# Softmax denominators over slots computed on VectorE through 32x32 block transposes, in a kernel of memory attention and a maxout feed-forward layer

## The chip, the cores and the metric

The kernel runs on one core of a Trainium2 chip. A core has TensorE (PE, matrix products into PSUM), VectorE (DVE), ScalarE (ACT), GpSimd (POOL) and SyncE (SP); each works through its own queue in order and waits for others by semaphores. Here POOL's queue issues nearly all loads and SP's queue the stores. The metric is the device time of one execution in microseconds; lower is better.

## The reference

Each of 8 x 8 (batch, head) pairs has 576 positions, 64 features and 32 memory slots. Weights over positions (`a`) gather keys and values into the 32 slots; queries then attend to the slots. The result, as 4608 tokens of 512 features, goes through a layer with the maximum of three products.

```python
a = np.exp(phi - np.max(phi, axis=2, keepdims=True))
a = a / (np.sum(a, axis=2, keepdims=True) + 1e-09)
k_m = np.einsum('bhsm,bhsd->bhmd', a, k)
v_m = np.einsum('bhsm,bhsd->bhmd', a, v)
scores = scale * np.matmul(q, k_m.transpose(0, 1, 3, 2))
attn = np.exp(scores - np.max(scores, axis=-1, keepdims=True))
attn = attn / (np.sum(attn, axis=-1, keepdims=True) + 1e-09)   # over the 32 slots
x = np.matmul(attn, v_m)                                       # then (4608, 512)
h = np.maximum(np.maximum(x @ w1, x @ w2), x @ w3)
out = h @ w_out
```

## The kernel before

The whole kernel is one list of steps, written out by hand in the text at the end of the function (lines 509 to 530) and emitted in that order. A step is a letter, an index and a batch, such as F6@1; a "!" at its end swaps the engine that empties its PSUM buffer, VectorE for ScalarE or the reverse (table EVAC, line 137). Every engine takes its own instructions from the list in that order. Pools decide when a buffer can be written again: four PSUM buffers of two banks serve all products, and k and v have one buffer for even and one for odd batches.

The algebra is rearranged: with x = attn v_m, the product x @ w1 is attn (v_m w1), so v_m is multiplied with the weights first ("fold"), and attn, already laid out with slots on partitions, is multiplied with that. The maximum with x @ w3 is taken by subtracting w3 from w1 and w2 beforehand and adding w3 w_out back at the end.

The steps, for batch b:

- H, L: loads of k, v (L94), phi (L90), q (L102). Y: weights (L108, L115). I: identity matrix on GpSimd. Z: warm-up products of zeros (L132).
- E: exponential of phi, ScalarE, L203. B: the gathering of keys and values into slots, 72 products for k and v of 32-wide tiles (L216); batch 1 splits it in B0 and B1. N: reciprocal and normalising on VectorE (L232, L236, L246). K: transposes of the result (L261).
- Q: queries transposed in 32x32 blocks on VectorE (L273), in two halves. S: scores (L295), then two exponentials on ScalarE, g = 0 and g = 1, into tile e2 (L304), where 128 partitions are four heads of 32 slots each.
- M: denominators, by a product with a block matrix of ones, so that every partition gets the sum of its 32 slots (L316). R: 1/sum as exp(-ln(sum)) on ScalarE (L329, L335). X: the product of e2 with it on VectorE, into tile attn (L340). All three once for each g.
- W, O, V: the transposed w3, the product w3 w_out and the differences of the weights, once (L157, L165, L186).
- D: the folds (L361), evacuated into wp; D3 goes with w3 w_out. F: twelve products per batch of attn with wp (L387); the even ones pass through a ReLU on ScalarE (L143), the odd ones through a maximum on VectorE (L400). T: the output product (L418, L427; T4 covers the seam of two batches, L436), a copy of PSUM to SBUF (L145 or L149) and a store.

Of the kernel before, what the change touches and what calls it, by code (L numbers as in the profile page):

```python
# [8 lines left out]
FP32 = mybir.dt.float32  # L9
BF16 = mybir.dt.bfloat16  # L10
AF = mybir.ActivationFunctionType
ALU = mybir.AluOpType
# [3 lines left out]
def kernel(  # L16
# [12 lines left out]
    nc = tc.nc  # L29

    B, H, S, D = q.shape
    M = phi.shape[-1]
    P = 128
    NP = H // 2
    NG = NP // 2
    HP = P // 2
    NC = S // HP
    R = 32
# [3 lines left out]
    SH = S // 2  # L42
    BANK = 512

    const = ctx.enter_context(tc.tile_pool(name="const", bufs=1))
    inp = ctx.enter_context(tc.tile_pool(name="inp", bufs=2))
    work = ctx.enter_context(tc.tile_pool(name="work", bufs=2))
# [3 lines left out]
    acc_pool = ctx.enter_context(  # L51
        tc.tile_pool(name="accp", bufs=4, space=bass.MemoryType.PSUM)
    )
# [28 lines left out]
    def load_ph(b):  # L82
        ph = inp.tile([P, NP, NC, M], FP32, name="ph")
        loaded.setdefault(b, {})["ph"] = ph
        dst = ph.rearrange("p j c m -> p j (c m)")
        if b == 0:
            for h in halves:
                nc.sync.dma_start(out=dst[:, h], in_=by_pair(phi, b)[:, h])
        else:
            nc.gpsimd.dma_start(out=dst, in_=by_pair(phi, b))  # L90

    def load_kv(b, i, h=slice(0, NP)):
        kv = loaded.setdefault(b, {})["kv"] = kvos[b % 2]
        nc.gpsimd.dma_start(  # L94
            out=kv[:, i, h].rearrange("p j c d -> p j (c d)"),
            in_=by_pair((k, v)[i], b)[:, h],
        )

    def load_q(b):
        qq = inp.tile([P, NP, NC, D], BF16, name="qq")  # L100
        loaded.setdefault(b, {})["q"] = qq
        nc.gpsimd.dma_start(  # L102
            out=qq.rearrange("p j c d -> p j (c d)"), in_=by_pair(q, b)
        )

    def load_w(i):
        w = (moe_w1, moe_w2, moe_w3)[i]
        nc.gpsimd.dma_start(  # L108
            out=w_sb[:, :, i], in_=w.rearrange("(j p) f -> p j f", p=P)
        )  # L110
# [3 lines left out]
    def load_wo():  # L114
        nc.gpsimd.dma_start(out=wo_sb, in_=moe_w_out.rearrange("(t p) c -> p t c", p=P))  # L115
# [3 lines left out]
    warm = const.tile([P, BANK], BF16, name="warm")  # L119
    nc.vector.memset(warm, 0.0)  # L120
    nc.vector.memset(kvos[0][:, 2], 1.0)
    blkones = const.tile([P, P], BF16, name="blkones")
    nc.vector.memset(blkones, 0.0)
    for i in range(P // M):
        nc.vector.memset(blkones[M * i : M * (i + 1), M * i : M * (i + 1)], 1.0)
    nc.vector.memset(kvos[1][:, 2], 1.0)

    def warm_up(n):
# [68 lines left out]
    st = {}  # L197

    def att_exp(b, js=slice(0, NP)):
        s = st.setdefault(b, {})  # L200
        if "e" not in s:
            s["e"] = work.tile([P, NP, NC, M], BF16, name="e")
        nc.scalar.activation(out=s["e"][:, js], in_=loaded[b]["ph"][:, js], func=AF.Exp)  # L203

    def att_kv(b, part=None):
        s = st[b]
        kvp = acc_pool.tile([P, NG, BANK], FP32, name="kvp", tag="acc")
        s["kvp", part] = kvp
        kv = loaded[b]["kv"]
        cols = {None: slice(0, 3), 0: slice(0, 3, 2), 1: slice(1, 2)}[part]  # L210
        nd = {None: 3 * D, 0: 2 * D, 1: D}[part]
        for c in range(NC):
            for j in range(NP):
                for a in range(NG):
                    r = slice(HP * a, HP * (a + 1))
                    nc.tensor.matmul(  # L216
                        kvp[M * j : M * (j + 1), a, 0:nd],
                        lhsT=s["e"][r, j, c, :],
                        rhs=kv[r, cols, j, c, :],
                        start=(c == 0),  # L220
                        stop=(c == NC - 1),
                        tile_position=(HP * a, M * j),
                    )
# [54 lines left out]
    attns = {}  # L278
# [29 lines left out]
                scale=0.125,  # L308
            )

    def att_sum(b, g):
        s = st[b]
        e2 = s["e2"]
        sm = acc_pool.tile([P, 2, BANK], FP32, name="sm", tag="acc")
        for h in range(2):
            nc.tensor.matmul(  # L316
                sm[:, h, 0:SH],
                lhsT=blkones,
                rhs=e2[:, g, h * SH : (h + 1) * SH],
                start=True,  # L320
                stop=True,
            )
        s["sm", g] = sm

    def att_rec(b, g):
        s = st[b]
        sm = s["sm", g]
        ln = work.tile([P, S], FP32, name="ln")
        nc.scalar.activation(  # L329
            out=ln.rearrange("p (h n) -> p h n", h=2),  # L330
            in_=sm[:, :, 0:SH],
            func=AF.Ln,
        )
        r = work.tile([P, S], FP32, name="r")
        nc.scalar.activation(out=r, in_=ln, func=AF.Exp, scale=-1.0)  # L335
        s["r", g] = r

    def att_mul(b, g):
        s = st[b]
        nc.vector.tensor_tensor(  # L340
            out=attns[b // 2][:, g, (b % 2) * S : (b % 2 + 1) * S],
            in0=s["e2"][:, g, 0:S],
            in1=s["r", g],
            op=ALU.mult,
        )

    wps, wp3s = {}, {}
# [134 lines left out]
    def issue(b, n, swap):  # L482

        i = int(n[1:]) if len(n) > 1 else None
        {
            "I": lambda: make_identity(nc, ident),
            "Y": lambda: load_w(i) if i < 3 else load_wo(),
            "L": lambda: load_ph(b) if i == 0 else load_q(b) if i == 3 else load_kv(b, i - 1),
            "H": lambda: load_kv(b, i % 2, halves[i // 2]),
            "E": lambda: [att_exp(b, h) for h in (halves if b == 0 else [slice(0, NP)])],  # L490
            "B": lambda: att_kv(b, i),
            "N": lambda: att_kv_norm(b, i),
            "K": lambda: att_kv_t(b, swap, i),
            "Q": lambda: att_q(b, i),
            "S": lambda: att_score(b),
            "M": lambda: att_sum(b, i),
            "R": lambda: att_rec(b, i),
            "X": lambda: att_mul(b, i),
            "D": lambda: fold(b, i, swap),
            "F": lambda: ffn1(b, i, swap),  # L500
            "T": lambda: ffn2(b, i, swap),
            "W": lambda: w3_t(i, swap),
            "O": lambda: w3_o(i, swap),
            "V": lambda: w_diff(i),
            "Z": lambda: warm_up(i),
        }[n[0]]()


    for w in """
        H3@0 H2@0 H1@0 H0@0 L3@0 E@0 Z48@0 B@0 Y2@0 N@0 Y3@0 Q0@0 Q1@0 I@0 Z4@0 K@0! Z8@0 S@0  # L510
        Z6@0 M1@0 R1@0 Y0@0 Y1@0 L0@1 M0@0 R0@0 W2@0 W1@0 W0@0 Z9@0 O0@0 X0@0 O1@0 X1@0 O2@0
        O3@0 L1@1 V1@0 V0@0 D1@0 D0@0! L3@1 D3@0 V2@0 F8@0 F10@0 F4@0 V4@0 F2@0 D2@0! F6@0!
        D4@0 F0@0 F3@0 F1@0 E@1 F5@0 F7@0 L2@1 F9@0 F11@0 B0@1 N0@1 T3@0 Q0@1 L1@2 L0@2 K0@1!
        T1@0 Q1@1 S@1 B1@1 N1@1 M0@1 L2@2 R0@1 K1@1 M1@1 X0@1 T0@0 R1@1 D1@1! L3@2 D0@1 D2@1
        E@2 X1@1 T2@0 F6@1! F10@1 F8@1 F7@1 F11@1 F0@1 F1@1 D3@1 B@2 F4@1 N@2 F9@1 L1@3 F5@1
        K@2! F2@1 Q1@2 F3@1 D3@2 L0@3 D2@2 T4@1! Q0@2 S@2 T0@1 M1@2 E@3 R1@2 M0@2 R0@2 T1@1!
        D0@2 L2@3 X1@2 D1@2! B@3 T2@1! L3@3 X0@2 L1@4 N@3 L0@4 F2@2 F6@2 Q1@3 Q0@3 F4@2 K@3
        F10@2 F0@2 F3@2 S@3 L2@4 F1@2 F8@2 L3@4 F11@2 M1@3 F7@2 R1@3 D3@3 E@4 D0@3! F9@2 T3@1
        F5@2 M0@3 R0@3 B@4 D2@3 D1@3! X1@3 N@4 L0@5 X0@3 T0@2! F0@3 F2@3 Q1@4 F4@3 Q0@4 L2@5
        F10@3 K@4 F6@3 F11@3 E@5 F3@3 D1@4! D0@4 T2@2! S@4 L1@5 F7@3 F8@3 F1@3 M0@4 F5@3 F9@3  # L520
        R0@4 X0@4 M1@4 R1@4 B@5 N@5 X1@4 D2@4 L3@5 D3@4 Q0@5 T2@3! K@5 F6@4 L3@6 F0@4 Q1@5 F4@4
        F7@4 S@5 F5@4 L0@7 F2@4 Q1@6 L0@6 Q0@6 F8@4 M1@5 R1@5 F1@4 E@7 F9@4 T1@2 F3@4 M0@5 R0@5
        L1@6 E@6 F10@4 T1@3 T3@3 X1@5 X0@5 F11@4 D3@5 D0@5 L2@6 B@6 D1@5! T0@3! N@6 L1@7 F2@5
        L2@7 F4@5 K@6 T4@3! S@6 B@7 D2@5 N@7 F3@5 F8@5 L3@7 F0@5 Q0@7 M0@6 R0@6 F1@5 T0@4! M1@6
        Q1@7 K@7 R1@6 T3@2 X0@6 X1@6 S@7 F5@5 F10@5 F6@5 F9@5 M1@7 R1@7 F7@5 X1@7 F11@5 M0@7
        R0@7 T3@4 X0@7 D2@7! D2@6 D0@7 T4@5! D1@6 D0@6 D1@7! T0@5! F0@7 F8@6 F4@6 F0@6 F6@6
        F9@6 F1@7 F10@6 F5@6 F11@6 F2@7 F6@7 F7@6 F2@6 F1@6 D3@6 D3@7 T1@4 F4@7 F3@6 F5@7 F3@7
        F8@7 F10@7 F11@7 F9@7 F7@7 T3@6 T1@5 T2@5! T2@7! T1@6 T0@7! T1@7 T2@6! T0@6! T2@4! T3@5
        T4@7! T3@7
    """.split():  # L530
        n, b = w.rstrip("!").split("@")
        issue(int(b), n, w.endswith("!"))
# [30 lines left out]
```

## Time and profile before

| what | us |
|---|---|
| median of 13 runs | 170.94 |
| lowest, highest | 170.37, 171.69 |
| the profiled execution | 171.2 |
| its span, first to last instruction | 169.4 |
| PE busy | 163.5 |
| ScalarE busy | 112.7 |
| VectorE busy | 86.3 |

A row of the groups gives line, engine, operation, output and inputs by name, shape and count, then busy time in us and the mean of one in ns, then the idle time before them and what ended it. PE's matmuls overlap one another, so the mean of one (286 ns for 288 columns) is longer than the step from one to the next; the step is read from the chain of waits, which lists pieces with start, length and count. The table of loads gives the time from an issue on the queue to the landing of its last byte. Positions in time are microseconds from the span's start.

### The profile page before, as it was taken

What the parts mean: (1) busy time and instruction counts of PE and PEld (TensorE: products, weight loads), DVE (VectorE), ACT (ScalarE), POOL (GpSimd) and SP (SyncE); (2) the same over time, 40 slices, a digit from 0 to 9 for tenths busy, and PEclk for the clock granted to TensorE, in tenths of its full rate; (3) what the DMA queues carried; (4) which work ended last, traced back from release to release, by engine and by line L of the source; (5) the groups of instructions that cost most, each with busy time, mean ns of one, the idle gap of its engine ahead of it and who ended that gap; (6) DMA issues with size and microseconds to landing.
All of it is one profiled execution on the core that took longest, in us unless ns stands there. A gap on an engine that the chain in (4) does not pass through costs nothing.

```text
span 169.4 us, 4692 instructions
## 1 busy us (share of the span) xinstructions
PE 163.5 (97%) x2035; PEld 91.3 (54%) x2035; DVE 86.3 (51%) x146; ACT 112.7 (67%) x170; POOL 28.4 (17%) x43
## 2 busy tenths in 40 slices
PE   7999999999899999999999999999999999999991
PEld 2444553573367446655576655574736857444450
DVE  6404175986458628688469863165861738000000
ACT  4101444853897898999999998697989682242420
POOL 7853111103303313100433100000000000000000
PEclk9999999999999999999999999999999999999999
DMA  5999999999999999999999999931113001243433
GB/s 152 157 203 210 207 209 258 230 208 251 277 227 290 242 222 312 267 267 244 235 224 350 244 208 234 263 117 64 62 68 124 0 4 62 88 160 132 181 124 126
DMA packets 21973, 31.77 MB, mean 187 GB/s; under 512 B 1216, under 2 KB 16576, under 8 KB 21952
## 3 DMA queue, kind: packets, MB, share of 16 engines
q0 software_dynamic: 16080, 21.43, 65.9%
q1 hardware_dynamic: 5728, 9.90, 16.5%
q8 instruction: 16, 0.26, 0.6%
q10 hardware_dynamic: 144, 0.13, 0.2%
q14 instruction: 5, 0.04, 0.1%
HBM read 39.32 MB, written 9.44 MB: 288 GB/s over the span
## 4 chain that ended last, share of the span: by engine, by line
PE 96%; DVE 1%; issue 1%; ACT 0%; ACTq 0%
PE acc L387 29%; PE po L418 28%; PE po L132 11%; PE po L427 8%; PE wps L361 5%; PE kvp L216 4%; PE po L165 3%; PE sm L316 2%; PE sc L295 2%; PE po L436 1%; PE kvtp L261 1%; PE po L459 1%; PE pt L157 1%; DVE kvn L236 0%; DVE kvn L246 0%
## 5 line engine op out<-in xcount | busy, mean ns | idle before, releaser
L387 PE MATMUL acc<-attn,wp 128*128 128x288 bf16 x384 | 52.2, 286 | 0.0
L418 PE MATMUL po<-wo_sb,hT 128*128 128x512 bf16 x210 | 51.2, 379 | 0.0
L400 DVE TENSOR_TENSOR hT<-acc,h 128x576 bf16<-128x576 f32 x48 | 34.8, 752 | 20.2 <-PE acc L387 19.1
L387 PEld LDWEIGHTS <-wp 128*128 128x128 bf16 x384 | 36.5, 98 | 13.0 <-issue 1.6
L145 ACT COPY ot<-po 128x512 f32<-128x512 f32 x31 | 18.2, 588 | 24.0 <-PE po L427 20.6
L418 PEld LDWEIGHTS <-hT 128*128 128x128 bf16 x210 | 19.5, 98 | 23.8 <-issue 3.5
L143 ACT ACTIVATE h<-acc 128x576 bf16<-128x576 f32 x46 | 27.5, 657 | 3.7 <-PE acc L387 3.6
L145 ACT CAST wp<-wps 128x1024 bf16<-128x1024 f32 x27 | 26.1, 1015 | 1.7 <-PE wps L361 1.7
L132 PE MATMUL po<-warm 128*128 128x512 bf16 x75 | 19.3, 416 | 1.2 <-DVE warm L120 1.2
L427 PE MATMUL po<-wp,attn 128*128 128x512 bf16 x62 | 18.4, 379 | 0.0
L132 PEld LDWEIGHTS <-warm 128*128 128x128 bf16 x75 | 7.6, 105 | 11.0 <-issue 3.2
L340 DVE TENSOR_TENSOR attn<-e,r 128x576 bf16<-128x576 bf16 x16 | 11.8, 752 | 2.7 <-PE po L427 1.4
L273 DVE STREAM_TRANSPOSE qT<-qq 128x576 f32<-128x576 f32 x16 | 11.7, 758 | 0.3 <-DMA qq<-in_q_dram 0.3
L329 ACT ACTIVATE ln<-sm 128x576 f32<-128x576 f32 x16 | 10.4, 647 | 1.5 <-PE sm L316 1.1
L335 ACT ACTIVATE r<-ln 128x576 f32<-128x576 f32 x16 | 10.9, 683 | 0.5
L304 ACT ACTIVATE e<-sc 128x576 bf16<-128x576 f32 x16 | 9.6, 662 | 2.2 <-PE sc L295 2.2
L476 DVE COPY ot<-po 128x256 f32<-128x256 f32 x1 | 0.4, 424 | 20.5 <-PE po L467 20.5
L203 ACT ACTIVATE e<-ph 128x1152 bf16<-128x1152 f32 (+1 forms) x9 | 9.5, 1061 | 1.6 <-DMA ph<-in_phi_dram 1.5
L94 POOL DMA_DIRECT2D kvo<-in_k_dram x9 | 6.7, 739 | 22.5 <-PE kvp L216 14.4
L427 PEld LDWEIGHTS <-attn 128*128 128x128 bf16 x62 | 6.1, 98 | 7.2
L102 POOL DMA_DIRECT2D qq<-in_q_dram x8 | 6.0, 746 | 22.0 <-DVE qT L273 16.5
L145 ACT COPY kvt<-kvtp 128x384 bf16<-128x384 bf16 (+1 forms) x3 | 1.3, 445 | 11.9 <-PE kvtp L261 11.9
(48 smaller groups left out, 118.4 us busy)
## 6 DMA issues: line engine op xcount, KB each, us to landing
out_dram<-ot SPq DMA_DIRECT2D x35, 256.0 KB, 2.7
qq<-in_q_dram POOLq DMA_DIRECT2D x8, 576.0 KB, 19.7
ph<-in_phi_dram POOLq DMA_DIRECT2D x7, 576.0 KB, 17.3
kvo<-in_k_dram POOLq DMA_DIRECT2D x7, 576.0 KB, 18.2
kvo<-in_v_dram POOLq DMA_DIRECT2D x7, 576.0 KB, 19.4
w_sb<-in_moe_w_dram POOLq DMA_DIRECT2D x3, 768.0 KB, 19.8
wo_sb<-in_moe_w_out_dram POOLq DMA_DIRECT2D x1, 768.0 KB, 17.4
ph<-in_phi_dram SPq DMA_DIRECT2D x2, 288.0 KB, 2.9
```

The source lines that it names most:

```text
L132: nc.tensor.matmul(po[:, 0:BANK], lhsT=warm[:, 0:P], rhs=warm, start=True, stop=True)
L143: nc.scalar.activation(out=out_, in_=in_, func=AF.Relu)
L145: nc.scalar.copy(out=out_, in_=in_)
L273: nc.vector.transpose(out=s["qT"][:, j].rearrange("p j c r e -> p (j c r e)").bitcast(FP32), in_=loaded[b]["q"][:, j].rearrange("p j c d - ...
L304: nc.scalar.activation(out=e2[:, a].rearrange("p (t r c) -> p t r c", t=2, c=NC), in_=sc[a][:, :, 0:SH].rearrange("p t (c r) -> p t r c", ...
L329: nc.scalar.activation(out=ln.rearrange("p (h n) -> p h n", h=2), in_=sm[:, :, 0:SH], func=AF.Ln,)
L335: nc.scalar.activation(out=r, in_=ln, func=AF.Exp, scale=-1.0)
L340: nc.vector.tensor_tensor(out=attns[b // 2][:, g, (b % 2) * S : (b % 2 + 1) * S], in0=s["e2"][:, g, 0:S], in1=s["r", g], op=ALU.mult,)
L387: nc.tensor.matmul(acc[:, h, 0:SH], lhsT=wps[b][:, g, w * DF + ft * P : w * DF + (ft + 1) * P], rhs=attn[:, g, c0 : c0 + SH], start=(g == ...
L400: nc.vector.tensor_tensor(out=hT[:, ft, (b % 2) * S : (b % 2 + 1) * S].rearrange("p (h n) -> p h n", h=2), in0=a, in1=s["h1", ft], op=ALU.max,
L418: nc.tensor.matmul(po, lhsT=hT[:, fc, c0 : c0 + P], rhs=wo_sb[:, fc, :], start=(n == 0), stop=False,)
L427: nc.tensor.matmul(po, lhsT=attn[:, g, c0 : c0 + P], rhs=wp3s[b][:, g, :], start=False, stop=(g == NG - 1),)
```

## The change

The denominators leave TensorE and ScalarE. X becomes five operations on VectorE: e2, read as pairs of bf16 in one fp32 word, is transposed in 32x32 blocks, which puts the 32 slots of a position along a row; a reduction sums them; a reciprocal of the 18 sums per partition follows; the row is multiplied with it; a second transpose brings the result back into attn. Steps M and R, and the matrix of ones, are gone. The list of steps is another one, too: 64 warm-up products in place of 75, identity ahead of the fourth piece of k and v, other positions for nearly all steps, and other "!" marks.

```diff
-    blkones = const.tile([P, P], BF16, name="blkones")
-    nc.vector.memset(blkones, 0.0)
-    for i in range(P // M):
-        nc.vector.memset(blkones[M * i : M * (i + 1), M * i : M * (i + 1)], 1.0)
...
-    def att_sum(b, g):
...
-    def att_rec(b, g):
...
     def att_mul(b, g):
         s = st[b]
+        e2 = s["e2"][:, g]
+        t = work.tile([P, S // HP, R, 2], BF16, name="t", tag=f"t{g}")
+        tf = t.rearrange("p n r e -> p (n r e)").bitcast(FP32)
+        tv = t.rearrange("p n r e -> p n e r")
+        nc.vector.transpose(out=tf, in_=e2.bitcast(FP32))
+        sm = work.tile([P, S // HP, 2], FP32, name="sm", tag=f"sm{g}")
+        nc.vector.tensor_reduce(out=sm, in_=tv, op=ALU.add, axis=mybir.AxisListType.X)
+        nc.vector.reciprocal(out=sm, in_=sm)
         nc.vector.tensor_tensor(
-            out=attns[b // 2][:, g, (b % 2) * S : (b % 2 + 1) * S],
-            in0=s["e2"][:, g, 0:S],
-            in1=s["r", g],
+            out=t,
+            in0=t,
+            in1=sm.unsqueeze(2).to_broadcast([P, S // HP, R, 2]),
             op=ALU.mult,
+        )
+        nc.vector.transpose(
+            out=attns[b // 2][:, g, (b % 2) * S : (b % 2 + 1) * S].bitcast(FP32), in_=tf
         )
...
-            "M": lambda: att_sum(b, i),
-            "R": lambda: att_rec(b, i),
             "X": lambda: att_mul(b, i),
```

The opening and two later parts of the list, before (-) and after (+); lines of the list are cut to what the prediction speaks of:

```diff
-        H3@0 H2@0 H1@0 H0@0 L3@0 E@0 Z48@0 B@0 Y2@0 N@0 Y3@0 Q0@0 Q1@0 I@0 Z4@0 K@0! Z8@0 S@0
-        Z6@0 M1@0 R1@0 Y0@0 Y1@0 L0@1 M0@0 R0@0 W2@0 W1@0 W0@0 Z9@0 O0@0 X0@0 O1@0 X1@0 O2@0
-        O3@0 L1@1 V1@0 V0@0 D1@0 D0@0! L3@1 D3@0 V2@0 F8@0 F10@0 F4@0 V4@0 F2@0 D2@0! F6@0!
+        H3@0 H0@0 H2@0 I@0 H1@0 E@0 Z38@0 B@0 L3@0 N@0 Y2@0 Z3@0 K@0 Q0@0 Q1@0 Z7@0 S@0 X0@0
+        Z6@0 W2@0! W0@0 Y3@0 Y0@0 W1@0 Z10@0 O1@0 O3@0 X1@0 V1@0 V0@0 O2@0 O0@0 D1@0 Y1@0 L0@1
+        D0@0! D3@0 V2@0 F10@0 V4@0 L1@1 F8@0 L3@1 F6@0 D2@0 F0@0! F2@0 D4@0 F3@0 F4@0 E@1 L2@1
...
-        T1@0 Q1@1 S@1 B1@1 N1@1 M0@1 L2@2 R0@1 K1@1 M1@1 X0@1 T0@0 R1@1 D1@1! L3@2 D0@1 D2@1
-        E@2 X1@1 T2@0 F6@1! F10@1 F8@1 F7@1 F11@1 F0@1 F1@1 D3@1 B@2 F4@1 N@2 F9@1 L1@3 F5@1
+        F1@0 F11@0 F7@0 L0@2 F9@0 F5@0 B0@1 T3@0 N0@1 L0@3 K0@1! Q0@1 T2@0! B1@1 Q1@1 S@1 E@2
+        L2@2 L1@2 L0@4 N1@1 K1@1 T1@0 X0@1 D0@1 D1@1! L3@2 T0@0! D3@1 L1@3 L2@3 L3@3 D2@1 X1@1
+        F6@1! F0@1 F1@1 F2@1 F4@1 F7@1 F5@1 E@3 F8@1 F3@1 F10@1 F11@1 F9@1 B@2 N@2 L0@5 Q0@2
+        T1@1 L1@4 E@4 K@2 T4@1! Q1@2 S@2 T2@1! D0@2 D1@2! T0@1! X0@2 D3@2 B@3 X1@2 D2@2 T3@1
+        N@3 F6@2 Q0@3 Q1@3 F0@2 F1@2 F8@2 F7@2 L2@4 F4@2 K@3 L3@4 L1@5 F10@2 F9@2 S@3 L2@5
+        F11@2 F2@2 E@5 F5@2 F3@2 D2@3 D1@3! X0@3 X1@3 T2@2! D0@3 B@4 N@4 D3@3 T0@2! Q1@4 T3@2
...
+        F11@5 S@6 T4@5! S@7 T3@5 D1@6! D1@7! X0@6 D3@7 T0@5! X0@7 T2@4! D0@7 D0@6 D2@7 T1@4
+        T1@5 X1@7 X1@6 F6@6 F8@6 F10@6 F2@7 F3@7 F0@6 F7@6 F9@6 F2@6 F3@6 F1@6 F4@7 F11@6 F10@7
```

## The prediction

> **What bounds the kernel now.** I read the page's busy line and its chain of waits first, then the costliest groups with shapes kept apart, then the timeline of the opening, then the chain in order of time, and last the load queue with its landings.
>
> ```profile
> PE 163.5 (97%) x2035; PEld 91.3 (54%) x2035; DVE 86.3 (51%) x146; ACT 112.7 (67%) x170; POOL 28.4 (17%) x43
> PE 96%; DVE 1%; issue 1%; ACT 0%; ACTq 0%
> ```
>
> TensorE (PE) is the path: 96% of the chain, with 0.74 us (42.25) and 0.3 us (43.5) as the only lulls after 30 us. So only what leaves PE's own stream, or makes PE wait, moves the end. In the chain, pieces of 12 matmuls of L387 are mostly 1.47 to 1.65 us (about 0.122 per 288 columns at best), and six of L418 with two of L427 take 1.72 (0.215 per 512 columns).
>
> ```profile
> L340 DVE TENSOR_TENSOR attn<-e,r 128x576 bf16<-128x576 bf16 x16 | 11.8, 752 | 2.7 <-PE po L427 1.4 <-ACT r L335 1.1
> L273 DVE STREAM_TRANSPOSE qT<-qq 128x576 f32<-128x576 f32 x16 | 11.7, 758 | 0.3 <-DMA qq<-in_q_dram 0.3
> L335 ACT ACTIVATE r<-ln 128x576 f32<-128x576 f32 x16 | 10.9, 683 | 0.5
> L329 ACT ACTIVATE ln<-sm 128x576 f32<-128x576 f32 x16 | 10.4, 647 | 1.5 <-PE sm L316 1.1
> L316 PE MATMUL sm<-e,blkones 128*128 128x288 bf16 x32 | 6.2, 286 | 0.0
> L186 DVE TENSOR_TENSOR w_sb<-w_sb 128x2048 bf16<-128x2048 bf16 x2 | 2.4, 1216 | 0.0
> L186 DVE TENSOR_TENSOR w_sb<-w_sb 128x1024 bf16<-128x1024 bf16 x2 | 1.4, 686 | 2.7 <-DMA w_sb<-in_moe_w_dram 2.7
> L232 DVE RECIPROCAL rden<-kvp 128x2 f32<-128x2 f32 x8 | 1.3, 166 | 11.8 <-PE kvp L216 11.8
> ```
>
> These rows are what goes (L316, L329, L335, and L340 in its present form) and the nearest prices of what comes. The two L186 rows give VectorE's fixed part: 1024 more elements cost 530 ns, so 1024 elements cost 530 of the 686 and 156 ns are fixed.
>
> ```profile
> 20.27 1.50 PE L157 MATMUL pt<-ident,w_sb 128*128 128x128 bf16 x24
> 23.60 5.34 PE L165 MATMUL po<-wo_sb,w3T 128*128 128x512 bf16 x24
> 26.98 1.83 DVE L186 TENSOR_TENSOR w_sb<-w_sb 128x1024 bf16<-128x1024 bf16 x2 [2.68 <-DMA w_sb<-in_moe_w_dram]
> 28.87 0.52 PE L361 MATMUL wps<-w_sb,kvt 64*32 64x256 bf16 x16
> ```
>
> The opening is set by landings. By issue plus time to landing, w3 is in at 4.95 + 14.8 = 19.75 (PE's transposes start at 20.27), wo at 5.69 + 17.4 = 23.1 (L165 at 23.60), w1 at 7.07 + 19.8 = 26.9 (VectorE at 26.98, D1@0 on PE at 28.87). The warm-up matmuls fill time between these.
>
> ```profile
> 90.19 0.75 POOL L94 DMA_DIRECT2D kvo<-in_v_dram  x1
> kvo<-in_v_dram POOLq DMA_DIRECT2D x1, 576.0 KB, 19.4
> 110.47 0.87 PE kvp L216 x72
> ```
>
> Batch 7's v lands at 90.19 + 19.4 = 109.6 and is used at 110.47, 0.9 us later. The DMA line of the page shows 9 in nearly every slice up to some 110 us. So a second clock runs under PE: the loads, one behind another, 2.7 to 4.3 us per 576 KB tensor.
>
> **What the Trainium skill says.** "VectorE: DVE Perf Modes", The perf-mode tier table: tensor_reduce has only the 1x program, even for bf16. No run here shows a reduce, so I price it by L340, a 1x row of the same 576 elements. The same page, The DRAIN you can't avoid: a semaphore between two chained Vector operations "costs nothing extra here". The trace nearly agrees: the reciprocal at 14.95 takes 0.17 and its dependent starts at 15.15, a gap of 30 ns. "TensorE: Matmul & The Clock Gate", What's actually happening: an idle window of about 3.4 us halves the array clock; here all stretches show 1.00, and no lull that I expect is that long. "DMA: Bandwidth & Descriptors", Issuing engines are not separate DMA queues: loads and stores share 16 engines. That agrees with the spread: a tensor takes about 2.8 us when no output store falls beside it and 3.5 to 4 where one does, some 0.75 us per store.
>
> **The change, part by part.**
>
> *PE.* The 32 products of L316 go. Four lie in the opening, before 28.87, which w1's landing holds, so they free nothing. The other 28 are in the chain as pieces of two at 0.24 us: 28 x 0.122 = 3.4 us off the path. Warm-ups fall from 75 to 64 (11 x 0.216 = 2.4 us), all before L165: nothing gained, since w3, wo and w1 still follow the same bytes. On POOL's queue identity now stands ahead of the fourth k/v piece and of q (0.5 us); the pieces land 1.4 us apart (8.5, 9.9, 11.3, 12.8) behind a full queue, which covers it. The opening keeps its 28.9; if the cover fails, D1@0 moves by at most that 0.5.
>
> *ScalarE.* Minus L329 and L335, 21.3 us. The order's swap marks hand it four output copies (0.588), three 1024-wide and one 512-wide wp casts, a w3T copy, and take two kvt copies away: about +5.6. Sum 112.7 - 21.3 + 5.6 = 97. It frees no time by itself, as PE does not wait for it now.
>
> *VectorE.* Each of 16 att_mul calls becomes five chained operations. Transpose of 288 fp32 words: 156 + 288 x 1.045 (from 758 at 576) = 457 ns, twice. Reduce over 576: 752. Reciprocal of 18: 183 if an element costs a cycle as in L340's slope; the same page (First, the fixed hardware budget) gives a repeat count of 8, by which I estimate 16 x 8.3 + 166 = 299 as the upper end. Product with a broadcast fp32 operand: 752, as L340 has an fp32 operand too. Four gaps of 30. Sum 2.72 us, upper 2.84, against 0.74 now: 16 x 1.98 = +31.7. Less the blkones memsets (0.45) and the swapped evacuations (4 x 0.692 + 0.684 + 3 x 1.216 + 0.686 - 2 x 0.349 = 7.1): 86.3 + 31.7 - 7.6 = 110 of 167 us. Bounds for the reduce: 455 (a 2x rate) to about 1,350 (twice its streaming part); I take 752.
>
> *Does VectorE fit under PE?* I added both engines' work between landmarks of the new order, PE by chain pieces (F 0.49, T 1.72 or 1.84, D 0.29 or 0.38, B 0.8, K 0.17, S 0.41), VectorE by its rows a little below their means, as neighbours overlap (maximum 0.71, Q 0.72, N 1.02). B@2 to B@4: PE 21.2, VectorE 9.9 + 4 X (X is one att_mul) = 20.8. B@5 to B@7: PE 27.1, VectorE 15.6 + 4 X = 26.5. From S@6 to F6@6, which needs all four att_mul of batches 6 and 7: PE 12.7, VectorE 0.66 for the first exponential + 4 X = 11.5. All fit, narrowly. One does not: from S@1 to F6@1 PE has 4.8 us (K1, T1@0, D0, D1, T0@0, D3, D2), while F6@1 needs exponential 0.66, N1 and K1's copy 0.6, and 2 X = 5.4, so 6.7: PE waits about 1.5 to 1.9 us there. The old chain of sum, logarithm, exponential and product had 5.7 us and showed no wait. Behind this VectorE block stand F's maxima (L400), which hold PSUM buffers; four of these exist, two microseconds of F work.
>
> *The loads.* Faster PE meets the same stream. Against B@b in the new order (36.98 for B0@1, then PE's sum times 73.5/71.5, the old stretch's measured over added): B@4 would start at 36.98 + 37.4 x 1.028 = 75.4. Before, v4 landed at 74.6; the new queue puts phi of batch 5 ahead of it (half a tensor, 1.7 us) and about one more store (0.75): 77.0. So PE waits 1.5 us, and the wait at F6@1 is inside it, as the landing is a fixed time. B@5: k5 and v5 at 86.1 + 1 = 87, PE at 87.2. B@7: v7 is now the last load, 113.3 + 0.75; PE at 36.98 + 74.5 x 1.028 + 1.5 = 115. No further wait. Behind B@7 stand 48.5 us of PE work (54.9 before), in which loads play no part.
>
> *Sum.* -3.4 (sums) + 1.5 (v4, with F6@1 inside) + 0 (warm-ups, opening) = -1.9. Span 169.4 - 1.9 = 167.5; that execution took 171.2, span and 1.8 around it. On the median 170.94 this is 169.0 us.
>
> **Rivals.** *Everything is kept.* v4 lands as early as before and the lulls at 42 go: -3.4, perhaps -4.4: 167.5 down to 166.5. For it: PE's chain is gapless now although loads have only 0.9 to 3 us of lead. Against: the F6@1 count.
> *VectorE becomes the bound, slower than before.* Place: the three stretches above. Their slack runs out at X = 2.98, 3.07 and 3.0 (PE's sums times 1.028 for the first two). Beyond, each 0.1 us in X costs 0.4 in each. The 3.4 gained is spent at 4 x (3X - 9.05) = 3.4, X = 3.3. A reduce at its upper bound gives X of 3.3 to 3.45; with X = 3.5 the deficits sum to 5.8 and the time is 170.94 + 2.4 = 173.3. For it: an unseen reduce with 18 runs of 32. Against: all 1x rows here cost 1.04 ns per element.
> *The loads take it all.* Landings slip by 3.4 instead of 1.5, through more stores ahead of k and v: 170.9. Against: stores ahead of B@7 grow only from 17 to 18.
>
> **How the numbers follow.** The sum above 0.45 (own range 168.0 to 170.2), everything kept 0.25, VectorE bound 0.18, loads take all 0.12. The range 166.6 to 172.4 leaves out the tails of the second and third. No change means within 0.2%, 0.34 us, about what this measurement can tell. Faster: 0.45 + 0.25 + 0.02 = 0.72; same 0.07, most of the last case; slower 0.21, the third and a quarter of the last.
>
> **What would show it.** No L316, PE's busy sum down by what the fewer warm-ups and sums took; X near 2.7 in the timeline; VectorE 108 to 113 us; D1@0 at 28.9; PE idle before F6@1 with VectorE's transpose as releaser, and before B@4 with the load of v; last B at 114 to 115. Wrong if D1@0 starts much earlier or later, if X passes 3.0, or if PE waits on VectorE in many places.

## The result

The changed kernel takes **169.44 us** (median of 11 runs, 169.2 to 170.21) against 171.02 for the kernel before (48 runs on the same chips): a ratio of **0.9913 [0.9898, 0.9927]**. The prediction was 169.0, faster. The median span fell from 169.15 (12 runs of the kernel before; 169.0 and 169.2 in two larger sets) to 167.7 us. The execution whose profile follows is the shortest on record, with a span of 167.4 and a time of 169.2.

First the page's busy line and its chain shares, of the kernel after:

```profile
PE 159.1 (95%) x1992; PEld 86.9 (52%) x1992; DVE 110.3 (66%) x198; ACT 98.8 (59%) x145; POOL 28.3 (17%) x43
...
PE 57%; DMA 20%; DVE 15%; issue 3%; POOL 2%; ACT 1%; POOLq 0%; ACTq 0%
```

TensorE lost the sums. VectorE went from 86.3 to 110.3 us and ScalarE from 112.7 to 98.8, against 110 and 97 in the prediction. The chain changed more than the time did: 96% of it was TensorE before, now 35% of it runs through a load of v and VectorE. A chain follows one releaser back at each step, so a wait of 0.26 us for batch 1's v is enough to lead it back along that load for 25.7 us. It says that several clocks are close together, not that 35% of the span is there to be won. By a clock I mean here a stream of work that can set the pace; TensorE's granted clock is another matter.

The costliest groups with shapes kept apart, VectorE, of the kernel after (count, busy us, mean ns, idle before):

```profile
L317 DVE TENSOR_TENSOR t<-t,sm 128x576 bf16<-128x576 bf16 x16 | 12.1, 758 | 0.5
L315 DVE TENSOR_REDUCE sm<-t 128x18 f32<-128x576 bf16 x16 | 12.0, 753 | 0.6
L323 DVE STREAM_TRANSPOSE attn<-t 128x288 f32<-128x288 f32 x16 | 7.7, 478 | 0.6
L313 DVE STREAM_TRANSPOSE t<-e 128x288 f32<-128x288 f32 x16 | 7.3, 454 | 4.0 <-ACT e L300 4.0
L316 DVE RECIPROCAL sm<-sm 128x18 f32<-128x18 f32 x16 | 4.3, 267 | 0.6
```

The five means add up to 2.71 us; start to start, one att_mul takes 2.75 to 2.80. Only the first step ever waits, for the exponential.

Where TensorE waited after the opening (us in total, times, longest), first before, then after:

```profile
PE kvp L216 <- issue: 0.7, 1, 0.7
```

```profile
PE acc L367 <- DVE attn L323: 1.4, 2, 1.2
PE sc L291 <- issue: 0.7, 2, 0.4
PE kvp L212 <- DMA kvo<-in_v_dram: 0.3, 1, 0.3
PE acc L367 <- DVE kvn L242: 0.2, 1, 0.2
```

Added up, 28 products of 0.122 us left the path, 3.4 us, and the named waits grew from 0.7 to 2.6. The difference, 1.5, is the size of the fall of the median span (169.15 - 167.7 = 1.45). It is not a closed account of these two traces. From D1@0 to the end the time fell only from 140.5 to 139.7, and the rest of the 2.0 between the two spans lies in the opening (see e8). So some 0.7 us was lost behind D1@0 in pauses that this list, which leaves out those under 0.15 us, doesn't show.

The waits stand in TensorE's timeline (start, us, and in brackets the idle time before and what ended it), after:

```profile
40.46 0.75 PE L212 MATMUL kvp<-kvo,e 64*32 64x64 bf16 x72 [0.26 <-DMA kvo<-in_v_dram]
...
41.77 0.46 PE L291 MATMUL sc<-qT,kvt 32*32 32x288 bf16 x25 [0.31 <-issue]
...
48.65 5.79 PE L367 MATMUL acc<-attn,wp 128*128 128x288 bf16 x46 [1.24 <-DVE attn L323]
...
76.10 0.93 PE L212 MATMUL kvp<-kvo,e 64*32 64x192 bf16 x72
...
91.53 0.33 PE L291 MATMUL sc<-qT,kvt 32*32 32x288 bf16 x10 [0.39 <-issue]
...
115.08 0.93 PE L212 MATMUL kvp<-kvo,e 64*32 64x192 bf16 x72
```

At 48.65 F6@1 waits for the second att_mul of batch 1. VectorE's timeline, after, shows that block without a hole, up to the 48.60 that TensorE waited for:

```profile
42.98 0.48 DVE L313 STREAM_TRANSPOSE t<-e 128x288 f32<-128x288 f32 x1 [0.32 <-ACT e L300]
...
45.77 0.43 DVE L313 STREAM_TRANSPOSE t<-e 128x288 f32<-128x288 f32 x1
46.24 0.75 DVE L315 TENSOR_REDUCE sm<-t 128x18 f32<-128x576 bf16 x1
47.03 0.27 DVE L316 RECIPROCAL sm<-sm 128x18 f32<-128x18 f32 x1
47.33 0.76 DVE L317 TENSOR_TENSOR t<-t,sm 128x576 bf16<-128x576 bf16 x1
48.12 0.48 DVE L323 STREAM_TRANSPOSE attn<-t 128x288 f32<-128x288 f32 x1
```

At 76.10 B@4 starts with no wait at all. Its v was issued on POOL's queue at 56.38; the DMA issues, after (KB, us to landing):

```profile
kvo<-in_v_dram POOLq DMA_DIRECT2D x1, 576.0 KB, 18.8
```

It was in at 75.2, 0.9 us before use. The wait that I had priced at 1.5 us is not there.

### The profile page after: what moved, and what is told of

It reads as the page before. It is cut to its first block, busy times and chain, and to the rows that moved or that the text cites. A ratio compares the mean times of both kernels' runs of the same rounds, so it can differ in the third digit from the quotient of the medians.

```text
span 167.4 us, 4624 instructions
## 1 busy us (share of the span) xinstructions
PE 159.1 (95%) x1992; PEld 86.9 (52%) x1992; DVE 110.3 (66%) x198; ACT 98.8 (59%) x145; POOL 28.3 (17%) x43
## 4 chain that ended last, share of the span: by engine, by line
PE 57%; DMA 20%; DVE 15%; issue 3%; POOL 2%; ACT 1%; POOLq 0%; ACTq 0%
PE acc L367 23%; DMA kvo<-in_v_dram 20%; PE po L398 19%; PE po L407 5%; DVE t L317 4%; DVE sm L315 4%; PE wps L341 3%; DVE attn L323 2%; PE kvp L212 2%; DVE t L313 2%; PE sc L291 2%; DVE sm L316 1%; PE po L416 1%; POOL kvo L94 1%; PE po L439 1%
## 5 line engine op out<-in xcount | busy, mean ns | idle before, releaser
L367 PE MATMUL acc<-attn,wp 128*128 128x288 bf16 x384 | 50.8, 286 | 1.6 <-DVE attn L323 1.4
L141 ACT COPY ot<-po 128x512 f32<-128x512 f32 x35 | 20.7, 591 | 28.9 <-PE po L407 24.3
L139 ACT ACTIVATE h<-acc 128x576 bf16<-128x576 f32 x46 | 28.5, 655 | 8.6 <-PE acc L367 7.5
L141 ACT CAST wp<-wps 128x1024 bf16<-128x1024 f32 (+1 forms) x31 | 29.7, 1015 | 0.9 <-PE wps L341 0.9
L128 PE MATMUL po<-warm 128*128 128x512 bf16 x64 | 17.3, 430 | 1.2 <-DVE warm L120 1.2
L317 DVE TENSOR_TENSOR t<-t,sm 128x576 bf16<-128x576 bf16 x16 | 12.1, 758 | 0.5
L315 DVE TENSOR_REDUCE sm<-t 128x18 f32<-128x576 bf16 x16 | 12.0, 753 | 0.6
L128 PEld LDWEIGHTS <-warm 128*128 128x128 bf16 x64 | 6.6, 108 | 9.9 <-issue 3.8
L90 POOL DMA_DIRECT2D ph<-in_phi_dram x7 | 5.3, 759 | 31.5 <-ACT e L199 27.4
L313 DVE STREAM_TRANSPOSE t<-e 128x288 f32<-128x288 f32 x16 | 7.3, 454 | 4.0 <-ACT e L300 4.0
```

What stands on the lines that cost most here:

```text
L128: nc.tensor.matmul(po[:, 0:BANK], lhsT=warm[:, 0:P], rhs=warm, start=True, stop=True)
L139: nc.scalar.activation(out=out_, in_=in_, func=AF.Relu)
L141: nc.scalar.copy(out=out_, in_=in_)
L313: nc.vector.transpose(out=tf, in_=e2.bitcast(FP32))
L315: nc.vector.tensor_reduce(out=sm, in_=tv, op=ALU.add, axis=mybir.AxisListType.X)
L317: nc.vector.tensor_tensor(out=t, in0=t, in1=sm.unsqueeze(2).to_broadcast([P, S // HP, R, 2]), op=ALU.mult,)
```

## The experiments

My theory: the sums on TensorE are worth 3.4 us, and about half is taken back because two clocks run close under TensorE, VectorE's softmax chain and the stream of loads. The rivals: only one of these two holds the time; or the sums were worth less; or the new list alone, or the shorter opening, made the gain. The new list with the old operations was not run. All results first, each in the median, its ratio to the kernel before with the 95% interval, and the median span.

| kernel | us | ratio | span |
|---|---|---|---|
| changed kernel | 169.44 | 0.9913 [0.9898, 0.9927] | 167.7 |
| e1 new operations, old list | 194.2 | 1.1367 [1.1328, 1.1406] | 192.4 |
| e2 changed, scores before B1@1 | 169.64 | 0.9931 [0.9906, 0.9957] | 167.9 |
| e3 changed, light att_mul | 169.59 | 0.9927 [0.9901, 0.9952] | 167.85 |
| e4 before, no sums | 169.35 | 0.9908 [0.9877, 0.9938] | 167.5 |
| e5 changed, fewer loads | 169.36 | 0.9923 [0.9896, 0.9949] | 167.3 |
| e6 changed, light att_mul, fewer loads | 168.23 | 0.9854 [0.9822, 0.9887] | 166.2 |
| e7 before, fewer loads | 171.38 | 1.0040 [1.0018, 1.0062] | 169.05 |
| e8 changed, 75 warm-ups | 169.75 | 0.9934 [0.9909, 0.9958] | 167.8 |
| e9 before, no sums, fewer loads | 167.95 | 0.9806 [0.9772, 0.9841] | 165.5 |
| e10 changed, softmax moved ahead | 170.23 | 0.9953 [0.9936, 0.997] | 168.5 |
| e11 e10, fewer loads | 169.89 | 0.9931 [0.9907, 0.9955] | 167.85 |

The five kernels with fewer loads have 2.0 to 2.45 us outside their span, the others 1.8. Why is open; nothing in a trace shows what lies outside it. So these five are compared by their spans. In the code cuts below, lines of the list are cut and joined to what moves.

**The operations without the list.** e1 takes the changed operations in the old list, with the M and R entries taken out. One line of it, against the kernel before:

```diff
-        Z6@0 M1@0 R1@0 Y0@0 Y1@0 L0@1 M0@0 R0@0 W2@0 W1@0 W0@0 Z9@0 O0@0 X0@0 O1@0 X1@0 O2@0
+        Z6@0 Y0@0 Y1@0 L0@1 W2@0 W1@0 W0@0 Z9@0 O0@0 X0@0 O1@0 X1@0 O2@0
...
```

> The new att_mul in the old list of steps (M and R deleted from it, nothing else moved). Theory A, the operations save PE work and the new list is needed to make room for them on VectorE: the 28 sums free 3.4 us, but the old places of X leave the five operations (2.7 us instead of 0.75) less PE work to hide behind, so PE waits for VectorE add 3 us or more and the ratio to before is 0.995 to 1.02. Theory B, the gain comes from the operations and the list matters little: ratio 0.985 to 0.993, like the changed kernel's 0.991. Theory C, the gain comes from the new list (its earlier opening): ratio above 1.0 with D1@0 at 28.9 us.

It took 23 us more than the kernel before, far outside the ranges of A and B; C, the earlier opening, is answered by e8. TensorE's longest waits in e1:

```profile
PE acc L367 <- DVE attn L323: 7.5, 3, 4.2
PE po L398 <- DVE hT L380: 3.8, 3, 1.7
PE acc L367 <- DVE rden L228: 3.3, 1, 3.3
```

The waits do not stop at TensorE's idle time. In e1 a piece of its timeline, and below it one stretch of the windows, whose columns are busy us (and instructions) of PE, PEld, DVE, ACT and POOL, then the granted clock:

```profile
83.96 0.59 PE L407 MATMUL po<-wp,attn 128*128 128x512 bf16 x2
88.73 4.02 PE L367 MATMUL acc<-attn,wp 128*128 128x288 bf16 x16 [4.18 <-DVE attn L323]
```

```profile
88.73:92.75 4.02, 4.02 (x18) 2.60 (x19) 1.27 (x2) 1.95 (x3) 1.49 (x2) 0.50 0.20 15
```

After 4.18 us of idleness the clock was 0.50, and 16 products took 4.02 us, 0.25 each where 0.122 is usual. The Trainium skill states half the clock after an idle window of about 3.4 us ("TensorE: Matmul & The Clock Gate", What's actually happening). This wait agrees with it, but the same trace has half the clock behind shorter waits too, as here behind one of 1.73 us, with one of 1.41 shortly before it:

```profile
145.95 2.72 PE L398 MATMUL po<-wo_sb,hT 128*128 128x512 bf16 x6 [1.73 <-DVE hT L380]
```

```profile
145.95:150.00 4.05, 4.05 (x26) 1.13 (x33) 3.74 (x7) 0.41 (x1) 0.00 (x0) 0.59 0.02 4
```

The granted clock of the whole run was 0.956. I estimate from it that some 8 us of the 23 are clock that was not granted ((1 - 0.956) x 192.9). The waits after the opening, 19.0 us in all, less the 3.4 of the sums, make up the rest. So the reorder is no extra of the change. The operations need it: without it TensorE stands behind VectorE's queue in many places.

**The VectorE chain alone.** e2 moves the scores of batch 1 ahead of B1@1, so that the exponential starts earlier.

```diff
-T2@0! B1@1 Q1@1 S@1 E@2
+T2@0! Q1@1 S@1 B1@1 E@2
```

> The changed kernel with Q1@1 and S@1 ahead of B1@1, so that batch 1's exponentials need not wait behind v's landing. Theory A, PE's wait of 1.24 us before F6@1 is VectorE's chain of two att_mul started too late: S@1 ends about 1.2 us earlier, the wait falls to 0.3 us or less, the time by about 1 us to a ratio near 0.985. Theory B, the landings of the loads set the pace after it: the wait goes but PE waits for a load later, the ratio stays at 0.991.

The wait at F6@1 fell, but only from 1.24 to 0.82, not to 0.3 or to nothing, and the time did not fall. TensorE's timeline and VectorE's, of e2:

```profile
42.29 0.29 PE L212 MATMUL kvp<-kvo,e 64*32 64x64 bf16 x25 [0.66 <-issue]
...
49.15 5.80 PE L367 MATMUL acc<-attn,wp 128*128 128x288 bf16 x46 [0.82 <-DVE attn L323]
```

```profile
42.73 0.29 DVE L232 TENSOR_TENSOR kvn<-kvp,rden 128x128 bf16<-128x128 f32 x1 [2.98 <-PE kvp L212]
```

The softmax stands on VectorE's queue behind N1@1, and N1@1 needs B1@1. With the exponential early, VectorE was idle for 2.98 us in front of that queue entry, and the second att_mul ended at 49.10, no earlier than the 48.60 of after. The wait is shorter only because TensorE itself came later: it had lost 0.66 us within B1@1 and 0.49 at K1@1, waiting for N1@1. An early operand gains nothing when something else stands ahead of it in the queue.

e3 takes away the reduce and the reciprocal: att_mul multiplies by a constant 1/32, so its output is not normalized, and one att_mul takes some 1.7 us.

```diff
-        sm = work.tile([P, S // HP, 2], FP32, name="sm", tag=f"sm{g}")
-        nc.vector.tensor_reduce(out=sm, in_=tv, op=ALU.add, axis=mybir.AxisListType.X)
-        nc.vector.reciprocal(out=sm, in_=sm)
+        sm = smc
```

> The changed kernel with the reduction and the reciprocal left out: att_mul multiplies with a constant, so the attention weights are not normalised over slots and each att_mul takes 1.7 us in place of 2.7. Theory A, what the changed kernel loses against the bare saving is waiting for VectorE: F6@1's wait and the smaller ones around 81, 91 and 104 us go, 1.5 to 2.5 us less, ratio 0.976 to 0.983. Theory B, landings hold it: PE arrives early and waits for k and v instead, ratio 0.988 to 0.992.

VectorE's work fell by 16 us, and TensorE's wait for it at F6@1 went. The time stayed. TensorE's timeline of e3:

```profile
87.04 0.94 PE L214 MATMUL kvp<-kvo,e 64*32 64x192 bf16 x72 [0.49 <-DMA kvo<-in_v_dram]
...
93.16 0.33 PE L293 MATMUL sc<-qT,kvt 32*32 32x288 bf16 x10 [1.40 <-issue]
```

Now B@5 waits for v, and a lull of 1.4 us stands in the scores of batch 4. VectorE did not hold the time by itself.

**The loads alone, and both.** e5 loads q for the first two batches only; later batches reuse these, so it leaves out six of eight q loads and answers the wrong queries there. The arithmetic stays. e6 does this and e3's edit together.

```diff
+        if b > 1:
+            loaded.setdefault(b, {})["q"] = loaded[b % 2]["q"]
+            return
```

> The changed kernel with the queries of batches 2 to 7 not loaded: they reuse those of batches 0 and 1, so six loads of 576 KB (some 17 us of the load stream) are gone and the output for these batches is of other queries. Theory A, VectorE's chains cost the changed kernel its remaining waits: little changes, 0 to 0.7 us less, ratio 0.987 to 0.992, F6@1 still waits 1.2 us. Theory B, the saturated loads hold it (landings of v, and PE's own instruction packets that queue behind them in the lulls near 41 and 91 us): 1.5 to 3 us less, ratio 0.974 to 0.983.

> The same with the reduction and the reciprocal left out as well (weights not normalised, queries of batches 2 to 7 reused). If VectorE's chain costs something that the loads had covered in e3, this is 1 us or more below e5; if the chain costs nothing even without the loads, both are equal within 0.4 us.

In span, the light att_mul alone is +0.15 us and fewer loads alone -0.4; together they are -1.5. The runs are few, but the spans lie apart: 166.1 to 167.0 in e6, 167.2 to 168.2 in e5, 167.5 to 168.4 in e3. That is the sign of two clocks side by side: each removal alone exposes the other. In e5 the wait at F6@1 still is 1.2 us. TensorE's waits after the opening, of e6:

```profile
PE sc L296 <- issue: 1.3, 2, 0.9
PE acc L370 <- ACT wp L146: 0.3, 1, 0.3
```

No wait for VectorE and none for a load is left, only lulls without a releaser and a short wait for ScalarE. The lulls are no part of what e6 gained. How the loads held e3 is shown only in part: of the 1.65 us of median span between e3 and e6, the two traces show 0.8 behind D1@0 (139.2 and 138.4 us to the end), the 0.49 for v in it.

**The price of the sums.** e4 is the kernel before with the sum products left out: the logarithm reads the exponential itself, so every denominator is replaced by the numerator. ScalarE and VectorE keep all their steps.

```diff
-        sm = acc_pool.tile([P, 2, BANK], FP32, name="sm", tag="acc")
-        for h in range(2):
-            nc.tensor.matmul(
...
+        sm = e2[:, g].rearrange("p (h n) -> p h n", h=2)
```

> The kernel before without the products with the matrix of ones: the logarithm on ScalarE reads the exponentials themselves, so the denominators are not summed; every operation of VectorE and ScalarE stays. Theory A, 28 of the 32 products stand in PE's gapless stream at 0.122 us each: 3.4 us less, ratio 0.980. Theory B, the loads' pace takes part of it: 1 to 2 us less, ratio 0.988 to 0.994, with waits for k or v on PE. The opening's four sums free nothing: D1@0 stays at 28.9 us.

The gain was 1.65 us of span, not 3.4. TensorE's timeline of e4 shows what took most of the rest:

```profile
109.23 0.94 PE L216 MATMUL kvp<-kvo,e 64*32 64x192 bf16 x72 [1.30 <-DMA kvo<-in_v_dram]
```

Batch 7's v came 0.9 us before its use in the kernel before; with faster products it came 1.3 too late. e7 and e9 are the kernel before and e4, both with e5's edit:

> The kernel before with the queries of batches 2 to 7 reused. Its PE stream shows lulls of only 0.74 and 0.3 us after 30 us, so both theories give 0 to 1 us less, ratio 0.994 to 1.000; more than that would mean that loads slow PE without an idle gap.

> The kernel before without the products with ones (the logarithm reads the exponentials, so denominators are not summed) and with the queries of batches 2 to 7 reused. Without the sums alone 1.6 us were gained, with PE waiting 1.3 us for batch 7's v. Theory A, the sums are worth 3.4 us in PE's stream and the loads kept part of it: 3 to 3.8 us below the kernel before with fewer loads (171.4), 167.6 to 168.4, span 165.4 or so, no wait for v. Theory B, the sums are worth only what e4 showed: 169.3 to 170.

e7 has the span of the kernel before (169.05): where nothing waits for loads, fewer of them are worth nothing. e9 has 165.5, and the difference is 3.55 us for the priced 3.4 (3.75 if each is set against the kernel before in its own comparison, 169.0 and 169.2). TensorE's timeline of e9 at the same place has no wait:

```profile
108.55 0.94 PE L219 MATMUL kvp<-kvo,e 64*32 64x192 bf16 x72
```

So the 3.4 us were there, and in this program the stream of loads allows about half of it. As e4 gains on the old list what the changed kernel gains, the new list need not be worth anything by itself; that it isn't was not tested.

**The opening.** In the profile of after D1@0 starts at 27.66, 1.2 us earlier than before. e8 restores the 75 warm-ups.

```diff
-        H3@0 H0@0 H2@0 I@0 H1@0 E@0 Z38@0 B@0 L3@0 N@0 Y2@0 Z3@0 K@0 Q0@0 Q1@0 Z7@0 S@0 X0@0
-        Z6@0 W2@0! W0@0 Y3@0 Y0@0 W1@0 Z10@0 O1@0 O3@0 X1@0 V1@0 V0@0 O2@0 O0@0 D1@0 Y1@0 L0@1
+        H3@0 H0@0 H2@0 I@0 H1@0 E@0 Z48@0 B@0 L3@0 N@0 Y2@0 Z4@0 K@0 Q0@0 Q1@0 Z8@0 S@0 X0@0
+        Z6@0 W2@0! W0@0 Y3@0 Y0@0 W1@0 Z9@0 O1@0 O3@0 X1@0 V1@0 V0@0 O2@0 O0@0 D1@0 Y1@0 L0@1
```

> The changed kernel with 48, 4, 8, 6 and 9 warm-up products at the old counts in place of 38, 3, 7, 6 and 10. Theory A, the opening follows the landings of w3, wo and w1 (D1@0 in the profiles so far 27.7 to 29.2 us with the very same opening list): no change, ratio 0.990 to 0.993. Theory B, the fewer warm-ups are what let the opening start 1.2 us earlier: ratio 0.996 to 1.000.

The time is the changed kernel's within the intervals, so the shorter opening did not make the gain. But the opening did depend on the warm-ups. TensorE's timelines of after, then of e8:

```profile
22.39 5.34 PE L161 MATMUL po<-wo_sb,w3T 128*128 128x512 bf16 x24 [0.21 <-DMA wo_sb<-in_moe_w_out_dram]
27.66 0.75 PE L341 MATMUL wps<-w_sb,kvt 64*32 64x256 bf16 x16
```

```profile
23.64 5.34 PE L161 MATMUL po<-wo_sb,w3T 128*128 128x512 bf16 x23
28.92 0.52 PE L341 MATMUL wps<-w_sb,kvt 64*32 64x256 bf16 x16
```

In both, D1@0 starts 5.3 us after the product w3 w_out. In after TensorE waited there for wo. In e8 wo was in at 22.5, but TensorE was busy with its own work until 23.64; the kernel before shows no wait there either. So eleven warm-ups less let D1@0 start about 1 us earlier when the loads are early (the 1.26 between the two, less some 0.2 by which wo and w1 landed earlier in after). With later loads they don't: kernels with after's warm-ups started D1@0 anywhere from 27.66 to 29.22 (e3, where wo landed at 23.8), the kernels on before's list from 28.30 to 28.87.

The early start is mostly taken back. From D1@0 to the end after takes 139.7 us and e8 138.7, and B@7 starts at 115.08 and 115.22. In after v1 lands at 40.4, and the wait for it (0.26) and both lulls (0.31, 0.39) are absent in e8.

**Can the wait at F6@1 be removed?** e10 moves the scores ahead of B1@1 as e2 does, X0@1 ahead of N1@1, and X1@1 ahead of the folds. K1@1 goes behind T1@0 and T0@0, with ScalarE to empty it. e11 is e10 with e5's edit.

```diff
-T2@0! B1@1 Q1@1 S@1 E@2 L2@2 L1@2 L0@4 N1@1 K1@1 T1@0 X0@1 D0@1 D1@1! L3@2 T0@0! D3@1 L1@3 L2@3 L3@3 D2@1 X1@1
+T2@0! Q1@1 S@1 B1@1 E@2 L2@2 L1@2 L0@4 X0@1 N1@1 T1@0 T0@0! K1@1! X1@1 D0@1 D1@1! L3@2 D3@1 L1@3 L2@3 L3@3 D2@1
```

> The changed kernel with batch 1's steps so placed that VectorE's chain starts as soon as the exponentials are there: Q1@1, S@1, B1@1, then X0@1 ahead of N1@1, T1@0 and T0@0 ahead of K1@1 (evacuated by ScalarE), X1@1 ahead of D0@1. Theory A, only the wait before F6@1 is at stake: it falls below 0.3 us and 1 us is gained, ratio 0.985. Theory B, two clocks: with the wait gone PE meets the loads of batch 5 and its lull near 91 us, as the light att_mul did: 0 to 0.5 us gained, ratio 0.989 to 0.993.

> The same with the queries of batches 2 to 7 reused. Under theory B this now gains what e10 does not: 0.8 to 1.3 us below e5, about 168.3 us; under the theory that the wait before F6@1 was harmless anyway it equals e5 and e10.

The wait of 1.24 us for VectorE went, and the kernel became 0.8 us slower than the changed one, outside both ranges above. TensorE's and ScalarE's timelines of e10:

```profile
47.42 0.62 PE L341 MATMUL wps<-w_sb,kvt 64*32 64x512 bf16 x16 [0.79 <-ACT kvt L141]
48.97 0.67 PE L367 MATMUL acc<-attn,wp 128*128 128x288 bf16 x4 [0.49 <-ACT wp L141]
```

```profile
47.91 3.76 ACT L141 CAST wp<-wps 128x1024 bf16<-128x1024 f32 x4 [0.53 <-PE wps L341]
```

K1, put later and emptied by ScalarE, delays the folds, and their four casts then stand in a row on ScalarE in front of F's products. e11 has the same waits and missed its forecast too: its span is 0.55 us above e5's, not 0.8 to 1.3 below. So e10 and e11 put a new wait in place of the old one and don't tell what the old one alone costs. No variant of the changed kernel that keeps all its loads beats it.

## The prediction, step by step

- *The sums, -3.4: right.* Shown by e9 against e7, 3.55.
- *One att_mul, 2.72 us: nearly right as a sum*, 2.75 to 2.80 with its gaps. Reduce 753 (752 predicted) and transposes 454 and 478 (457). The reciprocal of 18 elements was mis-sized: 267 ns, not 183. From 166 ns at 2 elements to 267 at 18 is 6.3 ns per element, where the transposes take about 1.05 (454 ns at 288, 761 at 576). The upper end (299) was the better guess.
- *VectorE fits, except at F6@1: right.* At F6@1 TensorE waited 1.24 for VectorE, a little less than the predicted 1.5 to 1.9. Its only later listed waits for VectorE are 0.21 (at 81.01) and 0.15 (at 104.71).
- *The wait for v4, +1.5: wrong.* I put v4's landing at 77.0, half a phi and a store behind the 74.6 of before; it was 75.2. I put TensorE's arrival at 75.4; it was 76.10, since the waits at v1 and F6@1 and the first lull lay before it. So B@4 had 0.9 us to spare. Half of the difference can lie in the execution, whose loads ran 0.9 us ahead from the opening on: in e3, where w1 came at 27.5, v4 landed at 76.4 (56.56 + 19.8). Even that held B@4 up by nothing. Where the rest went is not settled.
- *"F6@1 inside it": wrong with it.* I had let a wait in front of a fixed landing cost nothing. Without that landing F6@1 stood in the sum, with the lulls and v1: 1.9 us of added waits instead of 1.5. That the total came out so close is luck: a wait that did not occur stood in for others, of which the lulls and v1 were not foreseen. The idea behind it, that a faster TensorE runs into loads, is shown, by e4 and e3, at other batches.
- *Warm-ups and opening, 0: right at the end of the kernel (e8), wrong in its reason.* I read the opening as set by landings. But TensorE had no wait in it before from 8.7 us on, nor in e8 but for 0.16, and with fewer warm-ups D1@0 came 1.2 us earlier, which I had named as a sign of being wrong. It is worth nothing in the end because waits behind it take it back.
- *B@7 at about 115, and 48.5 us of TensorE work behind it: right*, 115.08 (115.22 in e8) and 48.6.
- *The rivals.* VectorE as the bound needed a slow reduce, and it was not slow. What this rival describes does exist: it is e1, the same operations in an order that does not make room for them. "Everything is kept" would have needed the loads and VectorE out of the way at once: e6's span is 2.95 below the kernel before's.

## What to carry to other kernels

When work moves from the bound engine to one with spare time, compare both engines' work between two dependent points of the order, not over the span: 110 us of 167 fitted in one list and cost 23 us in another. When a removal gives half of what it was priced at, look for a second clock; take it away together with the first, since each alone can give nothing (+0.15 and -0.4, but -1.5 together). An early landing is a margin, and a faster kernel spends it: 0.9 us early before, 1.3 late in e4.

## What was unexpected in the hardware

TensorE has lulls of 0.2 to 1.4 us in the midst of its smallest products, for which the trace names no releaser: 0.74 before (at 42.98), 0.31 and 0.39 after, 1.40 in e3. In the thirteen traces there are 16 such lulls after the opening, and each ended 2.2 to 2.6 us after a packet of the queue "q8 instruction" began. The windows of after, for half a microsecond that ends 2.0 us before its second lull does, and the queue within that stretch:

```profile
89.00:89.50 0.50, 0.50 (x4) 0.24 (x3) 0.50 (x1) 0.50 (x1) 0.00 (x0) 1.00 1.24 316
```

```profile
q8 instruction: 1, 0.02, 12.7%
```

Sixteen of sixteen are hardly chance, and it looks as if TensorE's supply of instructions came late. The cause isn't shown: no run varied it, most of these packets are followed by no lull, and e6 has one at the same place with fewer loads, which speaks against a queue behind data alone.
